# One attention step in each TensorE slot: moving steps, loads and the order of x's chunks

## The chip, the cores and the metric

The kernel runs on one core of one Trainium2 chip. The metric is the device time of one execution in microseconds (us), a median over runs; lower is better.

## What is computed

A landmark attention for 8 batches of 8 heads (576 tokens, 64 wide, 32 landmarks), a feed-forward layer on its output and a second layer with a maximum over three products. q and k are drawn eight times larger than the others.

```python
def _attn_ref(q, k, v):
    q_lm = q.reshape(B, H, m, S // m, D).mean(axis=3)
    k_lm = k.reshape(B, H, m, S // m, D).mean(axis=3)
    A = sm(q, k_lm); Bm = sm(q_lm, k_lm); C = sm(q_lm, k)    # softmax(a b^T / sqrt(D))
    Z = Bm.transpose(0, 1, 3, 2) / (norm1(Bm) * norminf(Bm) + 1e-06)
    for _ in range(6):
        Z = 2 * Z - Z @ Bm @ Z
    return A @ Z @ C @ v

x = attention output as (4608, 512)
h = x @ w_in                                                  # 512 -> 2048
x = where(h > 0, h, exp(min(h, 0)) - 1) @ w_out               # 2048 -> 512
h = maximum(maximum(x @ w1, x @ w2), x @ w3)                  # 512 -> 768
out = h @ w_out2                                              # 768 -> 512
```

(`sm`, `norm1` and `norminf` are shortened here.)

## The kernel before

The first phase does the attention and the first layer, the second phase the layer with the maximum. The first phase is a row of **slots**, 32 to a batch: two halves of 288 tokens, each with 16 values of f, a block of 128 of the 2048 hidden units. Batch b holds slots 32 b to 32 b + 31; below, a slot is named by its place in its batch, 0 to 31. A slot has

- `h_mm` (L667): six matmuls into one of two PSUM buffers `ph`, then on ScalarE a relu and an exp (L671, L672) into `eh`;
- the attention steps that the plan puts into this slot;
- `h_post`: VectorE finishes `eh` (L677), which frees `ph`; ScalarE casts it to the high part of `gt`, GpSimd subtracts for the low part (L103);
- `x_mm` (L698): twelve matmuls for the slot three before, three for each of the four chunks `x0` to `x3` of the output in PSUM. At the end of a half ScalarE copies chunks 0 and 2 and VectorE chunks 1 and 3 to `xo` (L724, L726), and the sync engine (SP) stores them to `xs`.

So the matmul of slot t + 2 waits for `eh` of slot t, and that of x in slot t + 3 for `gt` of slot t.

While batch b - 1 has its 32 slots, the attention of batch b is worked off as small **steps** inside them. `STEP_SLOTS` gives each step its slot, counted from the first slot of batch b - 1 (negative: before it); batch 1 has `SECOND_SLOTS`, `THIRD_SLOTS` overrides four entries of batch 2. The steps are: sums of q and k over landmarks on VectorE (q0, k0, q1, k1; L279), scores c0 and c1, `exp_t` for the two head groups (e0, e1), the product with v (cv0, cv1), the small softmax (b, b2), its norm (nb), `bbt`, six Newton steps n0 to n5, the scores of A (ah0, ah1) with their softmax in three parts (a10 to a31; casts `ah`, subtractions `al`), the small product m, and four W steps (`w_step`, slots in `W_SLOTS`) that make the batch's own first weight `wp`: 16 matmuls, two casts on ScalarE (L639), two subtractions on VectorE (L644).

`exp_t` transposes the exponentials: four chunks of 128 columns by four transposes into one PSUM bank, a copy by ScalarE (L463), then the last chunk of 64 columns into the other bank, and a copy by VectorE (L466). All attention steps share the two banks of the tile `banks`, in turn; every matmul and transpose of a step is issued through a helper, so its line is L235.

In the same slots the second layer's weights are converted. A `Narrowing` loads 1 MB of 64-bit words (L108) into the tile that also holds v, ScalarE widens them (L119, L122), VectorE shifts (L128), GpSimd adds (L131), and SP stores the result (L779). There are two in each of batches 1 to 6.

TensorE and VectorE issue in the order of the program from slot 20 of batch 0 on; ScalarE, GpSimd and SP issue in an order that the scheduler's planner chose when the program was built.

Of the kernel before, what the change touches and what calls it, by code (L numbers as in the profile page):

```python
# [19 lines left out]
def landmark_attention_mlp_maxout_kernel(  # L20
# [24 lines left out]
    CH = -(-S // P)  # L45
# [166 lines left out]
    state = {}  # L212
# [234 lines left out]
    def exp_t(b, g):  # L447
        e = state.pop(("e", b, g))
        if b == 0 and g:
            em = r_s.tile([P, CH - 1, P], F32, tag="gt", name="et", bufs=LAG + 1)  # L450
            el = r_s.tile([P, P], F32, tag="gt", name="et", bufs=LAG + 1)
        else:
            et = att.tile([P, CH, P], F32, tag="et", name="et")
            em, el = et[:, : CH - 1], et[:, CH - 1]
        pt = att_ps(b, "pe")
        for c in range(CH - 1):
            pt.put(
                nc.tensor.transpose,
                pt[:, c * P : (c + 1) * P],
                e[:, c * P : (c + 1) * P],  # L460
                ident,
            )
        nc.scalar.copy(em.rearrange("p c j -> p (c j)"), pt[:])  # L463
        p2 = att_ps(b, "pe")
        p2.put(nc.tensor.transpose, p2[:TAIL, :P], e[:, (CH - 1) * P :], ident)
        nc.vector.tensor_copy(el[:TAIL], p2[:TAIL, :P])  # L466
        state["et", b, g] = [em[:, c] for c in range(CH - 1)] + [el]

    def cv(b, g):
        et, vn, rs = state.pop(("et", b, g)), state["v", b], state["rs", b, g]  # L470
# [213 lines left out]
    def x_mm(b, half, f):  # L684
        gt = gts.pop((b, half, f))

        parts = b == 0
        first = f % (KF // 2) == 0 if parts else f == 0
        last = f % (KF // 2) == KF // 2 - 1 if parts else f == KF - 1
        if b == 0:  # L690
            conv.upto(index["out", f] + 1)
        if first:
            for ec in range(KD):
                xacc[ec] = ps_x.tile([P, 512], F32, tag=f"x{ec}", name=f"x{ec}")
        for ec in range(KD):
# [426 lines left out]
    def att_steps(b):  # L1122

        first = [
            ("q0", lambda: sums(b, 0, "q")),
            ("k0", lambda: sums(b, 0, "k")),
            ("q1", lambda: sums(b, 1, "q")),
            ("k1", lambda: sums(b, 1, "k")),
            ("c0", lambda: score_c(b, 0)),
            ("c1", lambda: score_c(b, 1)),  # L1130
            ("c20", lambda: score_c2(b, 0)),
            ("c21", lambda: score_c2(b, 1)),
            ("e0", lambda: exp_t(b, 0)),
            ("cv0", lambda: cv(b, 0)),
            ("e1", lambda: exp_t(b, 1)),
            ("b", lambda: soft_b(b)),
            ("b2", lambda: soft_b2(b)),
            ("cv1", lambda: cv(b, 1)),
            ("nb", lambda: norm_b(b)),
            ("bbt", lambda: bbt(b)),  # L1140
        ]
        for i in range(6):
            first.append((f"n{i}", lambda i=i: newton(b, i)))
        first += [("ah0", lambda: score_a(b, 0)), ("ah1", lambda: score_a(b, 1)), ("m", lambda: m_step(b))]
        for g in range(2):
            for n, fn in enumerate((soft_a1, soft_a2, soft_a3)):
                first.append((f"a{n + 1}{g}", lambda fn=fn, g=g: fn(b, g)))
        return first


    STEP_SLOTS = dict(
        q0=-10, k0=-9, q1=-8, k1=-6, c0=4, c1=5, b=6, b2=7, c20=8, c21=8, e0=8, nb=9, cv0=10, e1=11,
        ah0=12, cv1=13, bbt=13, ah1=14, n0=15, n1=16, n2=17, n3=18, n4=19, n5=20, m=22,
        a10=15, a11=16, a20=18, a21=19, a30=20, a31=21,
    )
    SECOND_SLOTS = dict(
        q0=3, k0=4, q1=5, k1=6, c0=8, c1=9, c20=11, c21=11, e0=12, b=10, b2=11, cv0=14, e1=15,
        nb=13, ah0=16, cv1=17, bbt=18, ah1=19, n0=20, n1=21, n2=22, n3=23, n4=24, n5=25, m=26,
        a10=20, a11=21, a20=23, a21=24, a30=25, a31=26,
    )  # L1160

    THIRD_SLOTS = dict(q0=-6, k0=-5, q1=-4, k1=-3)
    W_SLOTS = [-7, -5, -2, 1]
    SECOND_W = [-5, -3, -1, 2]

    def load_att(b):
# [71 lines left out]
    for _ in range(NF):  # L1238
# [13 lines left out]
        + [lambda i=i: newton(0, i) for i in range(6)]  # L1252
        + [lambda: m_step(0)],
        "V": [lambda: score_e(0)]
        + [lambda g=g, fn=fn: fn(0, g) for g in range(2) for fn in (score_c2, exp_t)]
        + [lambda g=g: cv(0, g) for g in range(2)],
        "A": [lambda h=h: score_a(0, h) for h in range(2)]
        + [
# [25 lines left out]
    def at(t, fn, *args):  # L1284
        plan[t].append((fn, args))
# [18 lines left out]
    for b in range(1, B):  # L1304
        t0 = (b - 1) * NSL
        if b > 1:
            at(t0 - (12 if b == 2 else 17), load_att, b)
            at(t0, load_v, b)
        for nm, stp in att_steps(b):
            if b > 1:  # L1310
                at(t0 + (THIRD_SLOTS.get(nm) if b == 2 and nm in THIRD_SLOTS else STEP_SLOTS[nm]), stp)
            else:
                at(SECOND_SLOTS[nm], after_post(stp))
        for n in range(NCH):
            at(t0 + NSL + (W_SLOTS if b > 1 else SECOND_W)[n], w_step, b, n)
# [147 lines left out]
```

## Time and profile before

| | us |
|---|---|
| median of 3 runs (1402.71 to 1405.16) | 1402.8 |
| the profiled execution | 1401.64 |
| its span, first to last instruction | 1399.8 |
| batch 0, to its last slot | 167.19 |
| batches 1 to 6 | 97.47, 99.60, 96.68, 96.45, 96.11, 96.30 |
| batch 7 (no attention beside it) | 77.13 |
| second phase | 572.87 |

Busy over the span: TensorE 94%, VectorE 60%, ScalarE 49%, GpSimd 48%. Times in the views count from the span's first instruction. An idle time in brackets is what the engine waited just before the row, and what ended that wait. Batch 3 starts at 364.26, batch 4 at 460.94.

### The profile page before, as it was taken

The numbers are of one execution on the slowest core, as the hardware profiler recorded it, in microseconds if no ns is written. First come the engines' busy times: TensorE is split into PE (matmuls) and PEld (weight loads), VectorE is DVE, ScalarE is ACT, GpSimd is POOL, SyncE is SP. The second block draws the span as 40 slices with busy tenths as digits, with TensorE's granted clock in tenths as the row PEclk, the third lists the DMA queues.
The fourth block names the chain that finished last, engine by engine and source line by source line (L and its number), as shares of the span: only waits on it lengthen the run. The fifth ranks groups of instructions, "written<-read, shape, count | busy, mean of one in ns | idle before, by whom it ended". The sixth has DMA issues, their size and how long they took to land.

```text
span 1399.8 us, 28302 instructions
## 1 busy us (share of the span) xinstructions
PE 1316.2 (94%) x11144; PEld 1233.9 (88%) x11144; DVE 841.9 (60%) x1603; ACT 682.8 (49%) x1555; POOL 677.8 (48%) x671
## 2 busy tenths in 40 slices
PE   4588999998999999999999999899999999999998
PEld 2477889888888888898899999899999999999998
DVE  6885646336346454364453458866777667687673
ACT  4784556555655656555566653322222222245451
POOL 2771424324325334233245457666666666685543
PEclk8698999999999999999999999999999999999999
DMA  9534104222222132041013112221222122249972
GB/s 361 217 108 151 35 19 160 67 72 90 66 99 70 59 130 81 18 161 63 35 63 108 48 63 73 84 97 67 86 109 83 54 110 84 78 151 314 296 246 76
DMA packets 91590, 152.30 MB, mean 109 GB/s; under 512 B 5312, under 2 KB 49472, under 8 KB 91456
## 3 DMA queue, kind: packets, MB, share of 16 engines
q1 hardware_dynamic: 91456, 150.49, 31.3%
q8 instruction: 87, 1.43, 0.4%
q14 instruction: 47, 0.39, 0.1%
HBM read 99.35 MB, written 51.12 MB: 107 GB/s over the span
## 4 chain that ended last, share of the span: by engine, by line
PE 69%; issue 7%; DMA 7%; ACT 6%; POOL 5%; DVE 5%; SPq 0%; POOLq 0%; ACTq 0%; DVEq 0%
PE p L986 24%; PE x L698 22%; PE ph L667 11%; PE p L1095 8%; PE banks L235 5%; DMA words<-in_moe_w_out_dram 3%; DMA words<-in_moe_w_dram 2%; POOL gt L103 1%; ACT words L122 1%; POOL u L854 1%; POOL wf L131 1%; DMA hf<-hs 1%; POOL w L951 1%; ACT eh L671 1%; ACT wf L119 1%
## 5 line engine op out<-in xcount | busy, mean ns | idle before, releaser
L698 PE MATMUL x<-gt,wo 128*128 128x288 f32 x3072 | 469.6, 302 | 11.4 <-DVE xo L726 3.4
L698 PEld LDWEIGHTS x<-gt,wo 128*128 128x128 f32 x3072 | 424.5, 189 | 52.6 <-ACT eh L671 21.8
L986 PE MATMUL p<-xo,w 128*128 128x256 f32 x3402 | 412.3, 284 | 6.9 <-ACT w L949 3.9
L986 PEld LDWEIGHTS p<-xo,w 128*128 128x128 f32 x3402 | 410.2, 191 | 8.9 <-ACT w L949 4.1
L103 POOL TENSOR_TENSOR gt<-eh,gt 128x288 fp32r<-128x288 f32 x243 | 195.9, 811 | 389.5 <-ACT gt L101 363.8
L667 PE MATMUL ph<-ah,wp 128*128 128x288 f32 x1024 | 250.0, 299 | 16.9 <-DVE eh L677 11.0
L667 PEld LDWEIGHTS ph<-ah,wp 128*128 128x128 f32 x1024 | 180.7, 191 | 26.1 <-DVE eh L677 15.7
L854 POOL TENSOR_TENSOR u<-s,v 128x512 f32<-128x512 f32 x99 | 136.2, 1375 | 134.6 <-DVE v L852 134.6
L677 DVE SCALAR_TENSOR_TENSOR eh<-eh,ph 128x288 f32<-128x288 f32 x256 | 113.1, 443 | 133.9 <-ACT eh L672 132.6
L671 ACT ACTIVATE eh<-ph 128x288 f32<-128x288 f32 x256 | 104.3, 409 | 175.9 <-PE ph L667 127.1
L667 PE MATMUL ph<-al,wp 128*128 128x288 f32 x512 | 152.8, 298 | 2.1 <-POOL al L103 2.1
L101 ACT CAST gt<-eh 128x288 fp32r<-128x288 f32 x256 | 109.3, 428 | 75.9 <-DVE eh L677 75.1
L843 ACT COPY s<-p 128x512 f32<-128x512 f32 x99 | 57.9, 585 | 175.2 <-PE p L986 148.5
L1095 PE MATMUL p<-wo,ho 128*128 128x256 f32 x1134 | 138.1, 284 | 4.1 <-ACT ho L1083 3.4
L1095 PEld LDWEIGHTS p<-wo,ho 128*128 128x128 f32 x1134 | 137.3, 192 | 4.8 <-ACT ho L1083 3.8
L672 ACT ACTIVATE eh<-eh 128x288 f32<-128x288 f32 x256 | 113.3, 444 | 5.4
L667 PEld LDWEIGHTS ph<-al,wp 128*128 128x128 f32 x512 | 97.3, 190 | 2.5 <-POOL al L103 2.5
L867 DVE TENSOR_TENSOR t<-p,u 128x512 f32<-128x512 f32 x81 | 55.7, 687 | 65.5 <-POOL u L854 63.2
L644 DVE TENSOR_TENSOR wp<-banks,wp 128x512 fp32r<-128x512 f32 x62 | 39.9, 685 | 76.1 <-ACT wp L639 76.1
L993 DVE TENSOR_TENSOR t<-t 128x1024 f32<-128x1024 f32 x54 | 71.7, 1328 | 9.0 <-POOL t L857 3.9
L1085 DVE TENSOR_TENSOR ho<-hf,ho 128x768 fp32r<-128x768 f32 x54 | 65.9, 1245 | 16.6 <-ACT ho L1083 16.3
L1083 ACT CAST ho<-hf 128x768 fp32r<-128x768 f32 x63 | 51.5, 835 | 42.9 <-PE p L1095 23.4
(167 smaller groups left out, 1421.1 us busy)
## 6 DMA issues: line engine op xcount, KB each, us to landing
hf<-hs SPq DMA_DIRECT2D x63, 384.0 KB, 5.2
hs<-t SPq DMA_DIRECT2D x27, 512.0 KB, 2.6
xs<-xo SPq DMA_DIRECT2D x36, 288.0 KB, 3.2
hs<-s SPq DMA_DIRECT2D x27, 384.0 KB, 2.9
qT<-in_q_dram SPq DMA_DIRECT2D x16, 576.0 KB, 6.1
kT<-in_k_dram SPq DMA_DIRECT2D x16, 576.0 KB, 7.1
words<-in_moe_w_dram SPq DMA_DIRECT2D x9, 1024.0 KB, 6.4
xf<-xs SPq DMA_DIRECT2D x9, 1024.0 KB, 5.0
```

What stands on the lines that cost most here:

```text
L101: nc.scalar.copy(hi, src)
L103: eng.tensor_tensor(out=lo, in0=src, in1=hi.bitcast(F32), op=ALU.subtract)
L235: ins = fn(*args, **kw)
L667: nc.tensor.matmul(ph[:, :HF], a, c, start=(g == 0 and j == 0), stop=(g == 1 and j == 2))
L671: nc.scalar.activation(e, ph[:, :HF], AF.Relu, scale=-1.0)
L672: nc.scalar.activation(e, e, AF.Exp, scale=-1.0)
L677: state["post"] = nc.vector.scalar_tensor_tensor(out=e, in0=e, scalar=1.0, in1=ph[:, :HF], op0=ALU.subtract, op1=ALU.max)
L698: nc.tensor.matmul(xacc[ec][:, :HF], a, gt[:, c], start=(first and j == 0), stop=(last and j == 2),)
L854: nc.gpsimd.tensor_tensor(out=u57, in0=s57, in1=v.unsqueeze(1).to_broadcast([P, 2, 256]), op=ALU.add)
L986: nc.tensor.matmul(dst, l, r, start=(c == 0 and j == 0), stop=(c == 1 and j == 2))
L993: nc.vector.tensor_tensor(out=t, in0=t, in1=cur, op=ALU.max)
L1095: nc.tensor.matmul(dst, l, r, start=(c == 0 and n == 0), stop=(c == NP - 1 and n == 2))
```

## The change

- `exp_t` is cut in two: the last chunk's transpose and its copy become a step of their own, `exp_t2` (t0, t1). In batch 0's own attention, ahead of the slots, the two still follow each other.
- The tables: in batches 2 to 7 no slot holds two steps that issue on TensorE. bbt moves from 13 to 10, cv0 from 10 to 11, e1 to 12, cv1 to 14, the A scores to 16 and 18, the Newton steps to 15, 17 and 19 to 22, m to 24, A's softmax to 19 to 25. The sums of q and k move from 22, 23, 24 and 26 to 24, 25, 26 and 28, the first two W steps from 25 and 27 to 26 and 28. In batch 1 only t0 and t1 are added.
- q and k of batches 3 to 7 are loaded in slot 19 instead of 15. The words are loaded in slots 15 and 23 instead of 13 and 24, and widened four slots later instead of three.
- `x_mm` takes the chunks in the order 0, 2, 1, 3.

```diff
@@ exp_t
+        state["et", b, g] = e, el, [em[:, c] for c in range(CH - 1)] + [el]
         pt = att_ps(b, "pe")
...
         nc.scalar.copy(em.rearrange("p c j -> p (c j)"), pt[:])
+
+    def exp_t2(b, g):
+
+        e, el, state["et", b, g] = state["et", b, g]
         p2 = att_ps(b, "pe")
         p2.put(nc.tensor.transpose, p2[:TAIL, :P], e[:, (CH - 1) * P :], ident)
         nc.vector.tensor_copy(el[:TAIL], p2[:TAIL, :P])
-        state["et", b, g] = [em[:, c] for c in range(CH - 1)] + [el]
@@ x_mm
-        for ec in range(KD):
+
+        for ec in (0, 2, 1, 3):
@@ 
     STEP_SLOTS = dict(
-        q0=-10, k0=-9, q1=-8, k1=-6, c0=4, c1=5, b=6, b2=7, c20=8, c21=8, e0=8, nb=9, cv0=10, e1=11,
-        ah0=12, cv1=13, bbt=13, ah1=14, n0=15, n1=16, n2=17, n3=18, n4=19, n5=20, m=22,
-        a10=15, a11=16, a20=18, a21=19, a30=20, a31=21,
+        q0=-8, k0=-7, q1=-6, k1=-4, c0=4, c1=5, b=6, b2=7, c20=8, c21=8, e0=8, t0=9, nb=9, bbt=10,
+        cv0=11, e1=12, t1=13, cv1=14, n0=15, ah0=16, n1=17, ah1=18, n2=19, n3=20, n4=21, n5=22, m=24,
+        a10=19, a11=20, a20=22, a21=23, a30=24, a31=25,
     )
@@ 
-    W_SLOTS = [-7, -5, -2, 1]
+    W_SLOTS = [-6, -4, -2, 1]
@@ 
-            at(t0 - (12 if b == 2 else 17), load_att, b)
+            at(t0 - (12 if b == 2 else 13), load_att, b)
@@ 
-        t0 = (1 + it // 2) * NSL + (13, 24)[it % 2]
+        t0 = (1 + it // 2) * NSL + (15, 23)[it % 2]
         at(t0, nw.load)
         run = nw.run()
         for n in range(4):
-            at(t0 + 3 + n, next, run, None)
+            at(t0 + 4 + n, next, run, None)
```

**TensorE, slots 8 and 9 of a batch.** `ident,e` are the transposes. First the order before, from the transposes of slot 8 to the next slot's first matmuls:

```order
L235 MATMUL banks<-ident,e 128x128 x4
L235 MATMUL banks<-ident,e 64x128
L698 MATMUL x_2023<-gt,wo 128x288 x3
L698 MATMUL x_2024<-gt,wo 128x288 x3
L698 MATMUL x_2025<-gt,wo 128x288 x3
L698 MATMUL x_2026<-gt,wo 128x288 x3
L667 MATMUL ph<-ah,wp 128x288
```

and TensorE in the same place of the changed kernel, to the lone transpose:

```order
L235 MATMUL banks<-ident,e 128x128 x4
L703 MATMUL x_2023<-gt,wo 128x288 x3
L703 MATMUL x_2025<-gt,wo 128x288 x3
L703 MATMUL x_2024<-gt,wo 128x288 x3
L703 MATMUL x_2026<-gt,wo 128x288 x3
L671 MATMUL ph<-ah,wp 128x288
L671 MATMUL ph<-al,wp 128x288
L671 MATMUL ph<-ah,wp 128x288 x2
L671 MATMUL ph<-al,wp 128x288
L671 MATMUL ph<-ah,wp 128x288
L235 MATMUL banks<-ident,e 64x128
```

The 64-column transpose has moved behind the twelve matmuls of x and the next slot's six.

**ScalarE, around the widening of the second words** (`wf<-words`), from the exp ahead of it. Before, in slot 20, with m's copy (`mt`) and no W step near:

```order
L672 ACTIVATE eh<-eh 128x288
L101 CAST gt<-eh 128x288
L119 ACTIVATE wf_2963<-words_2848 128x512
L122 ACTIVATE words_2848<-words_2848 128x512
L119 ACTIVATE wf_2966<-words_2848 128x512
L122 ACTIVATE words_2848<-words_2848 128x512
L101 CAST ah<-af 128x288 x2
L671 ACTIVATE eh<-ph 128x288
L101 CAST gt<-eh 128x288
L672 ACTIVATE eh<-eh 128x288
L101 CAST ah<-af 128x288 x2
L627 COPY mt<-banks 128x128
```

ScalarE in the changed kernel, in slot 24, to the casts of slot 26's W step (`wp`):

```order
L122 ACTIVATE words_2795<-words_2795 128x512
L101 CAST ah<-af 128x288 x2
L675 ACTIVATE eh<-ph 128x288
L101 CAST gt<-eh 128x288
L676 ACTIVATE eh<-eh 128x288
L101 CAST ah<-af 128x288 x2
L675 ACTIVATE eh<-ph 128x288
L101 CAST gt<-eh 128x288
L676 ACTIVATE eh<-eh 128x288
L643 CAST wp<-banks 128x512 x2
```

The widening now stands two slots ahead of a W step instead of five.

**VectorE, slots 24 to 29**: eh, the sums of q and k (L279), W's subtractions (`wp`), the shift (`wf`). Before:

```order
L279 TENSOR_REDUCE qs<-qT 128x64
L677 SCALAR_TENSOR_TENSOR eh<-eh,ph 128x288
L644 TENSOR_TENSOR wp<-banks,wp 128x512 x2
L677 SCALAR_TENSOR_TENSOR eh<-eh,ph 128x288
L279 TENSOR_REDUCE kT<-kT 128x2x32
L677 SCALAR_TENSOR_TENSOR eh<-eh,ph 128x288
L644 TENSOR_TENSOR wp<-banks,wp 128x512 x2
L677 SCALAR_TENSOR_TENSOR eh<-eh,ph 128x288
L128 TENSOR_SCALAR wf_2963<-wf_2963 128x512
L128 TENSOR_SCALAR wf_2966<-wf_2966 128x512
L677 SCALAR_TENSOR_TENSOR eh<-eh,ph 128x288 x2
```

and VectorE in the changed kernel, from slot 25's eh:

```order
L681 SCALAR_TENSOR_TENSOR eh<-eh,ph 128x288
L648 TENSOR_TENSOR wp<-banks,wp 128x512 x2
L279 TENSOR_REDUCE qs<-qT 128x64
L681 SCALAR_TENSOR_TENSOR eh<-eh,ph 128x288 x2
L648 TENSOR_TENSOR wp<-banks,wp 128x512 x2
L279 TENSOR_REDUCE kT<-kT 128x2x32
L128 TENSOR_SCALAR wf_2945<-wf_2945 128x512
L128 TENSOR_SCALAR wf_2948<-wf_2948 128x512
L681 SCALAR_TENSOR_TENSOR eh<-eh,ph 128x288 x2
```

W's subtractions, a sum and, in slot 28, the shift now stand together ahead of one eh.

## Rows read from the trace of the kernel before

**Rows 1.** Busy by stretch, one batch each (2, 4): stretch, us, engines' busy (instructions), granted clock, DMA

```profile
264.66:364.26 99.60, 93.74 (x828) 84.58 (x827) 47.94 (x119) 55.76 (x139) 34.47 (x42) 1.00 0.24 79
460.94:557.39 96.45, 93.33 (x828) 84.50 (x827) 47.56 (x119) 55.84 (x139) 34.46 (x42) 1.00 0.25 83
```

**Rows 2.** Waits of TensorE, whole span: who waited for whom, total us, times, longest

```profile
PE ph L667 <- DVE eh L677: 11.0, 11, 2.6
PE banks L235 <- ACT et L463: 8.3, 12, 0.9
...
PE x L698 <- DVE xo L726: 3.4, 6, 0.6
```

**Rows 3.** Busy by stretch, slots 8, 9, 10, 13, 15, 19, 22, 27

```profile
483.19:487.02 3.83, 3.15 (x25) 2.92 (x24) 2.58 (x13) 2.11 (x6) 2.20 (x4) 1.00 0.00 0
487.02:489.43 2.41, 2.41 (x20) 2.41 (x19) 1.93 (x8) 0.86 (x2) 0.58 (x1) 1.00 0.00 0
489.43:492.86 3.43, 3.43 (x60) 3.08 (x59) 0.75 (x3) 1.72 (x4) 1.18 (x2) 1.00 0.02 5
499.89:504.22 4.33, 3.92 (x65) 3.50 (x64) 1.48 (x5) 1.11 (x4) 0.80 (x1) 1.00 0.26 61
507.48:510.33 2.85, 2.85 (x24) 2.85 (x23) 0.42 (x1) 2.82 (x8) 0.72 (x1) 1.00 0.77 275
422.66:426.31 3.65, 3.11 (x24) 2.87 (x23) 3.16 (x10) 1.57 (x6) 2.81 (x4) 1.00 0.54 167
431.58:435.51 3.93, 3.12 (x25) 2.55 (x23) 0.51 (x2) 3.93 (x12) 1.84 (x3) 1.00 0.04 13
446.46:450.08 3.62, 3.62 (x36) 2.62 (x35) 0.90 (x3) 2.10 (x5) 1.55 (x2) 1.00 0.02 5
```

**Rows 4.** Timeline of TensorE: start, us, row, [idle before, its end]

```profile
485.26 0.30 PE L235 MATMUL banks<-ident,e 128*64 128x128 f32 x1 [0.68 <-ACT et L463]
...
425.01 1.47 PE L698 MATMUL x<-gt,wo 128*128 128x288 f32 x9 [0.54 <-DVE xo L726]
...
435.51 0.40 PE L667 MATMUL ph<-ah,wp 128*128 128x288 f32 x1 [0.81 <-DVE eh L677]
```

**Rows 5.** Timeline of ScalarE: second words in batches 3 and 2, first words, wp

```profile
430.93 0.69 ACT L119 ACTIVATE wf<-words 128x512 f32<-128x512 f32 x1 [2.36 <-DMA words<-in_moe_w_dram]
...
435.45 0.26 ACT L627 COPY mt<-banks 128x128 f32<-128x128 f32 x1
...
334.28 0.67 ACT L119 ACTIVATE wf<-words 128x512 f32<-128x512 f32 x1 [4.14 <-DMA words<-in_moe_w_dram]
...
506.88 0.68 ACT L119 ACTIVATE wf<-words 128x512 f32<-128x512 f32 x1 [0.72 <-DMA words<-in_moe_w_dram]
...
448.55 1.07 ACT L639 CAST wp<-banks 128x512 fp32r<-128x512 f32 x2
```

**Rows 6.** Timeline of SP's queue: issue of the second and of the first words

```profile
424.42 0.38 SPq L108 DMA_DIRECT2D words<-in_moe_w_dram  x1
...
501.74 0.37 SPq L108 DMA_DIRECT2D words<-in_moe_w_dram  x1
```

**Rows 7.** Timeline of VectorE: eh of slot 16, then slots 18 and 25 to 28

```profile
515.37 0.45 DVE L677 SCALAR_TENSOR_TENSOR eh<-eh,ph 128x288 f32<-128x288 f32 x1
...
420.35 1.15 DVE L128 TENSOR_SCALAR wf<-wf 128x512 uint32<-128x512 uint32 x2
...
445.23 1.34 DVE L279 TENSOR_REDUCE kT<-kT 128x64 f32<-128x1152 f32 x1
...
449.65 1.29 DVE L644 TENSOR_TENSOR wp<-banks,wp 128x512 fp32r<-128x512 f32 x2 [2.72 <-ACT wp L639]
450.86 0.45 DVE L677 SCALAR_TENSOR_TENSOR eh<-eh,ph 128x288 f32<-128x288 f32 x1
451.22 0.76 DVE L128 TENSOR_SCALAR wf<-wf 128x512 uint32<-128x512 uint32 x2
```

**Rows 8.** Timeline of GpSimd, the row beside the shift at 420.35

```profile
420.08 0.81 POOL L103 TENSOR_TENSOR gt<-eh,gt 128x288 fp32r<-128x288 f32 x1 [2.13 <-ACT gt L101]
```

More of the change, by code (lines that the diff above doesn't have):

```diff
@@ L1133, in att_steps @@
             ("e0", lambda: exp_t(b, 0)),
+            ("t0", lambda: exp_t2(b, 0)),
             ("cv0", lambda: cv(b, 0)),
             ("e1", lambda: exp_t(b, 1)),
+            ("t1", lambda: exp_t2(b, 1)),
             ("b", lambda: soft_b(b)),
             ("b2", lambda: soft_b2(b)),
-            ("cv1", lambda: cv(b, 1)),
             ("nb", lambda: norm_b(b)),
             ("bbt", lambda: bbt(b)),
+            ("cv1", lambda: cv(b, 1)),
         ]
@@ L1157, in landmark_attention_mlp_maxout_kernel @@
         q0=3, k0=4, q1=5, k1=6, c0=8, c1=9, c20=11, c21=11, e0=12, b=10, b2=11, cv0=14, e1=15,
-        nb=13, ah0=16, cv1=17, bbt=18, ah1=19, n0=20, n1=21, n2=22, n3=23, n4=24, n5=25, m=26,
+        nb=13, ah0=16, cv1=17, bbt=18, ah1=19, t0=13, t1=16, n0=20, n1=21, n2=22, n3=23, n4=24, n5=25, m=26,
         a10=20, a11=21, a20=23, a21=24, a30=25, a31=26,
@@ L1254, in landmark_attention_mlp_maxout_kernel @@
         "V": [lambda: score_e(0)]
-        + [lambda g=g, fn=fn: fn(0, g) for g in range(2) for fn in (score_c2, exp_t)]
+        + [lambda g=g, fn=fn: fn(0, g) for g in range(2) for fn in (score_c2, lambda b, g: [exp_t(b, g), exp_t2(b, g)])]
         + [lambda g=g: cv(0, g) for g in range(2)],
```

## The prediction

> **What bounds the kernel now.** I read the busy times in stretches first, one stretch for a batch. Batches 1 to 6 take about 96.5 us each, batch 2 99.6, with TensorE busy for some 93.5 of them at a granted clock of 1.00 and every other engine below 60 [rows 1]. So TensorE's own queue sets the time there, and only what makes it wait, or what it must do, counts. Batch 0 (167 us) and the second phase (573 us) are touched only at their edges.
>
> Second, the same view with one slot in each stretch [rows 3]. A slot without an attention step takes 2.41 us (18 matmuls). A step of four 128x128 matmuls makes it 2.85, the product with v 3.43, a W step 3.62. The stretches that don't fit these prices are the slots with two steps (8: 3.83; 13: 4.33), slot 19 (3.65 where a Newton slot is 2.85) and slot 22 (3.93, whose step is again four small matmuls).
>
> Third, what TensorE waited for [rows 2], and the waits in place [rows 4]. The last chunk's transpose stands 0.68 behind ScalarE's copy of the four others, 12 times, 8.3 us in all. In slot 19 the second chunk of x waits 0.54 for VectorE's copy out. At the end of slot 22 the next slot's first matmul waits 0.81 for VectorE's eh, because ScalarE had stood 2.36 us for the second words and made everything behind them late [rows 5].
>
> **What the change takes away**, per batch of 1 to 6 unless said.
>
> Transposes apart: slots 8 and 9 take 3.83 + 2.41 now. Four transposes alone are priced like four Newton matmuls, 2.85. The single one alone lies between a quarter of that step's 0.44 and all of it; I take 0.3, so 2.71, because entering and leaving a step costs too. Saved: 6.24 - 5.56 = 0.68. Slot 11 has the same pair and the same wait (12 waits are two per batch). 2 x 0.67 x 6 = 8.0 us. bbt alone: slot 13 and an empty one take 4.33 + 2.41, cv1 alone and bbt alone 3.43 + 2.85; saved 0.46, six times 2.8. Together **10.8**.
>
> Slot 19's wait: 3.65 - 2.85 = 0.8. In the new table slot 18 has only a score step and VectorE reaches the copies of x right after eh, while fifteen matmuls (15 x 2.41 / 18 = 2.0 us) lie between a chunk's last matmul and its next first. The wait goes even without the new chunk order; the order itself delays both the finish and the next need of each chunk equally, so I price it at nothing in these batches. **4.7**.
>
> Slot 22's wait: 3.93 - 2.85 = 1.08, six times 6.5. Batch 2 takes 99.60 where others take 96.5 [rows 1], since there both words transfers came later (4.14 us of wait instead of 2.36 [rows 5]); q and k now load after the first words have landed and x's store goes out ahead of the second, so I count these 3.1 as gone. **9.6**. Sum of gains: **25.1 us**.
>
> **What it adds.** The same engines now hold other work in other slots, and eh(t) must be done two slots later, when its PSUM buffer is written again.
>
> D, slot 20: VectorE now has a Newton pair, the second softmax pair and the narrowing's shift ahead of eh(20). Before, a Newton and a softmax pair ended 5.04 after their slot's start (515.37 against 510.33 [rows 3, 7]), part of it lateness from the slot ahead. With the shift (1.15) and eh (0.45) that is 6.6 against 2 x 2.85 = 5.7: 0.85 at most, nothing if the lateness is gone. I take 0.45, six times: **2.7**.
>
> F, slot 28: W's subtractions, k1's sum and the second shift now stand ahead of eh(28). The subtractions began 3.19 after a W slot's start and eh stood 1.21 behind them (446.46, 449.65, 450.86); the k sum takes 1.3, the shift 0.76, eh 0.45 [rows 3, 7]. Sum 6.9, against 3.62 + 2.41 = 6.0 until slot 30's first matmul: 0.9. Nothing there is late before, so no slack hides it. If the shift takes its other duration, 1.15, it is 1.3. q and k are summed in batches 1 to 5 only: 5 x 0.9 = **4.5**.
>
> The row of the shift that took 1.15 has a GpSimd subtraction beside it (420.08 [rows 8]); the one of 0.76 has none. The Trainium skill ("SBUF — State Buffer", section "SBUF: two separate sides") says that VectorE and GpSimd share one port pair as an exclusive lock, so that the later one blocks for the whole instruction. By that rule the crowded slot 28, where GpSimd has its own backlog, pays the long shift, F is 1.3 and the sum 2.0 worse. The trace agrees with the direction, not with a full block of 0.81.
>
> E, slot 26: W's subtractions and q1's sum ahead of eh(26). Without lateness that is 3.19 + 1.21 + 1.3 + 0.45 = 6.15 against 6.03: 0.1. But ScalarE widens the second words in slot 24. From the first widening to the end of the second pair of ah casts it took 4.52 (430.93 to 435.45 [rows 5]). ScalarE was free for it 2.26 after its slot's start (430.93 - 2.36 - 426.31), about 2.1 now. If the words are there, it is through 6.6 after slot 24's start; some 1.0 for relu, cast and exp, 1.07 for the wp casts (448.55), 1.21, 1.3 and 0.45 on VectorE make 11.65 against 2.85 + 2.41 + 3.62 + 2.41 = 11.3 until slot 28: 0.35. GpSimd's al subtractions, which hold the eh buffers, add up to 0.4; I take 0.5 plus the wait w for the words. Now w: the words were issued 4.07 after the shift's start (420.35 to 424.42 [rows 6, 7]). The shift starts about 4.8 into slot 20, so the issue is at 8.9 there, slot 24 starts at 11.35, and the transfer takes 5.1 (501.74 to 506.88) to 6.5 (424.42 to 430.93). Landing is 2.6 to 4.0 into slot 24, w is 0.4 to 1.8, and I take the middle, 1.0. E = 1.5, between 0.1 and 2.7; five times 7.5, and 0.2 in batch 6, which has no q1: **7.7**.
>
> The second words again, by a page: the Trainium skill ("DMA: Bandwidth & Descriptors", section "Bandwidth") gives 6.15 us for 1 MB. By that w would be 1.5 and the sum 3 us worse; the rows hold durations on both sides of it.
>
> G, batch 0: there VectorE adds the chunks in the order 0, 1, 2, 3 while TensorE now wants chunk 2 second, a chunk's three matmuls (0.4) earlier: **0.4**, at most twice.
>
> Costed at nothing: cv0, e1, cv1 and the Newton steps a slot later (every step still has its predecessor's result a slot earlier); q and k loaded at slot 19 instead of 15 (the first 0.6 MB is wanted five slots, some 13 us, later, the last nine slots later, and the words' 1 MB takes 6.5 at most); W steps in other slots (same matmuls); the moved stores of x on SP's queue, which nobody waits for until the next half.
>
> **Sum.** 25.1 - 2.7 - 7.7 - 4.5 - 0.4 = 9.8. The profiled execution took 1401.6 and lies 1.2 under the median of 1402.8; 1401.6 - 9.8 + 1.2 = **1393.0 us**.
>
> **Rivals.**
> 1. The words come in time and GpSimd is out of the way: E is 0.1 to 0.35 and the time 1386. For it: with q, k and x's stores elsewhere the words have the queues nearly alone, as in the 5.1 us transfer. Against: the stores of the first narrowing still go just ahead of them. 0.22.
> 2. Slower: the second words land late in every batch as they did in batch 2 (1.8 later than in the others), w is 2.8, E grows by 1.8 six times and the long shift stands in slot 28 (1.75): 1405.6. It decides from w of about 2.6. For it: ScalarE's queue still holds the widening ahead of casts and relus that TensorE needs. Against: that lateness shows in one batch. 0.08.
> 3. The change does not do what it says: the single transpose waits for the copy in its own slot too. 12 x 0.69 come back, 1401.3. Against it: the copy had ended when the transpose started at 485.26 [rows 4], and a lone transpose stands a slot later. 0.04.
> 4. D, E and F all come out at their long ends short of rival 2: 1397 to 1401. 0.16.
>
> **How the numbers follow.** My forecast, 1389 to 1397, has 0.50. With all additions at their low ends it is 1381, with D, E and F long and batch 2's 3.1 still there it is past 1405. The range 1382 to 1401 leaves out rival 2, rival 3's half and the tails, some 0.17. About 0.2% (2.8 us) is what a measurement here can tell: faster than 1400 has 0.86, within 0.2% 0.08 (rival 3 and the worst of 4), slower 0.06.
>
> **What would show it.** Right: no wait of TensorE for L463's copy or for x's copies in slot 19; slots 8, 9 and 10 near 2.85, 2.7 and 2.85; new waits for eh ahead of slots 28 and 30 in batches 1 to 5, none or little in batch 6, a small one ahead of slot 22. Wrong: slots 26 to 30 without any wait (E and F fall, about 1382), a single-transpose slot near 3.4, or a wait of ScalarE for words above 2.5 us.

## The result, and the profile after

The changed kernel takes 1388.3 us (median of 5 runs, 1387.5 to 1391.0), the kernel before in the same runs 1402.7: a ratio of 0.9908, 95% interval 0.9892 to 0.9924. The forecast was 1393.0 us with a range of 1382 to 1401. The profiled execution took 1388.28 us (before 1401.64), its span is 1386.5.

By stretch, in us, batches as in the table of before: batch 0 168.16; batches 1 to 6 96.12, 94.63, 96.65, 94.60, 94.30, 92.21; batch 7 77.15; second phase 572.7. So all of the gain lies in batches 1 to 6, 14.1 us, and 1.0 of it is lost in batch 0. The busy times of batches 4 and 6 (columns as in [rows 1]):

```profile
455.56:550.16 94.60, 92.86 (x828) 84.59 (x827) 47.70 (x119) 55.83 (x140) 34.43 (x41) 1.00 0.25 84
...
644.46:736.67 92.21, 92.21 (x828) 84.39 (x827) 42.96 (x115) 56.24 (x140) 34.52 (x42) 1.00 0.18 63
```

Batch 6, which has no sums of q and k, has no idle time of TensorE left: 92.21 of 92.21. Batch 4 waits 1.74 us in all, where before it waited 3.12 [rows 1]. The same view by slot, of batch 4, answers to [rows 3]: slots 8, 9, 10, 14, 19, 22, 24, 27 and 29.

```profile
477.81:480.66 2.85, 2.85 (x25) 2.85 (x23) 1.66 (x8) 1.69 (x5) 1.26 (x3) 1.00 0.00 0
480.66:483.18 2.52, 2.52 (x21) 2.50 (x20) 1.31 (x8) 1.29 (x3) 1.48 (x2) 1.00 0.00 0
483.18:486.05 2.87, 2.87 (x24) 2.87 (x23) 2.48 (x10) 1.34 (x4) 0.52 (x1) 1.00 0.00 0
494.77:498.20 3.43, 3.43 (x60) 3.08 (x59) 0.64 (x2) 1.72 (x4) 1.18 (x2) 1.00 0.12 19
510.52:513.37 2.85, 2.85 (x24) 2.85 (x23) 1.80 (x5) 1.23 (x4) 0.81 (x1) 1.00 0.94 350
519.08:522.09 3.01, 3.01 (x24) 2.94 (x23) 2.22 (x7) 1.17 (x4) 3.01 (x4) 1.00 0.32 117
524.50:527.46 2.96, 2.96 (x25) 2.62 (x23) 2.89 (x6) 1.76 (x5) 1.08 (x2) 1.00 0.57 219
533.48:537.11 3.63, 2.58 (x20) 2.34 (x18) 2.96 (x5) 1.51 (x5) 0.87 (x2) 1.00 0.00 0
540.83:544.04 3.21, 2.58 (x21) 2.34 (x19) 3.21 (x7) 0.88 (x3) 0.68 (x1) 1.00 0.00 0
```

The slots that lost their second step cost what their step costs, the lone transpose (slot 9) only 0.11 over an empty slot. Slots 19 and 22 have lost their waits but for 0.2 in 22. What is new is at the end: 27 and 29 are empty slots (2.41) that take 3.63 and 3.21, with TensorE busy for 2.58 in both and VectorE for all of slot 29. In batches 1 to 6 slot 27 takes 4.12, 3.85, 4.38, 3.63, 3.45, 2.41, slot 29 3.22, 3.21, 3.13, 3.21, 3.19, 2.41.

The waits of TensorE over the whole span (as [rows 2]) keep one large row of the slots. The rows for ScalarE's copy of the transposes (L463) and for VectorE's copies of x in slot 19 (L726) are gone, and that for eh has grown from 11.0 us to 15.1:

```profile
PE ph L671 <- DVE eh L681: 15.1, 17, 1.8
```

In place, in batch 3, at the end of slots 27 and 29, TensorE's timeline (start, us, row, idle before and what ended it):

```profile
441.07 0.43 PE L671 MATMUL ph<-ah,wp 128*128 128x288 f32 x1 [1.80 <-DVE eh L681]
...
449.44 0.40 PE L671 MATMUL ph<-ah,wp 128*128 128x288 f32 x1 [0.56 <-DVE eh L681]
```

VectorE's timeline there: W's subtractions, q's or k's sum, in slot 28 the shift, and eh last, twice, since it is two behind:

```profile
438.10 1.29 DVE L648 TENSOR_TENSOR wp<-banks,wp 128x512 fp32r<-128x512 f32 x2 [2.66 <-ACT wp L643]
439.31 1.34 DVE L279 TENSOR_REDUCE qs<-qT 128x64 f32<-128x1152 f32 x1
440.57 0.81 DVE L681 SCALAR_TENSOR_TENSOR eh<-eh,ph 128x288 f32<-128x288 f32 x2
...
445.80 1.29 DVE L648 TENSOR_TENSOR wp<-banks,wp 128x512 fp32r<-128x512 f32 x2 [4.43 <-ACT wp L643]
447.01 1.34 DVE L279 TENSOR_REDUCE kT<-kT 128x64 f32<-128x1152 f32 x1
448.27 0.75 DVE L128 TENSOR_SCALAR wf<-wf 128x512 uint32<-128x512 uint32 x2
448.94 0.81 DVE L681 SCALAR_TENSOR_TENSOR eh<-eh,ph 128x288 f32<-128x288 f32 x2
```

What W's subtractions waited for in slot 26 is on ScalarE, whose timeline shows the wait for the second words, smaller than before (2.36, [rows 5]), and a wait for GpSimd:

```profile
430.89 0.67 ACT L119 ACTIVATE wf<-words 128x512 f32<-128x512 f32 x1 [1.20 <-DMA words<-in_moe_w_dram]
...
436.03 0.41 ACT L675 ACTIVATE eh<-ph 128x288 f32<-128x288 f32 x1 [0.49 <-POOL gt L103]
...
437.01 1.06 ACT L643 CAST wp<-banks 128x512 fp32r<-128x512 f32 x2
```

### The profile page after: what moved, and what is told of

Read it like the earlier page. It is cut to its first block, busy times and chain, and to the rows that moved or that the text cites. A ratio compares the mean times of both kernels' runs of the same rounds, so it can differ in the third digit from the quotient of the medians.

```text
span 1386.5 us, 28338 instructions
## 1 busy us (share of the span) xinstructions
PE 1315.8 (95%) x11144; PEld 1235.8 (89%) x11144; DVE 839.5 (61%) x1603; ACT 684.5 (49%) x1555; POOL 678.2 (49%) x671
## 4 chain that ended last, share of the span: by engine, by line
PE 70%; issue 7%; DVE 6%; POOL 6%; DMA 5%; ACT 5%; SPq 0%; POOLq 0%; ACTq 0%; DVEq 0%
PE p L991 24%; PE x L703 21%; PE ph L671 11%; PE p L1100 9%; PE banks L235 5%; DMA words<-in_moe_w_out_dram 2%; DMA words<-in_moe_w_dram 2%; POOL gt L103 1%; POOL u L859 1%; DVE wp L648 1%; ACT words L122 1%; DMA hf<-hs 1%; POOL al L103 1%; ACT wp L643 1%; POOL w L956 1%
## 5 line engine op out<-in xcount | busy, mean ns | idle before, releaser
L671 PE MATMUL ph<-ah,wp 128*128 128x288 f32 x1024 | 252.3, 301 | 20.7 <-DVE eh L681 15.1
L131 POOL TENSOR_TENSOR wf<-wf,words 128x512 uint32<-128x512 uint32 x40 | 54.5, 1377 | 43.0 <-DVE wf L128 41.3
```

What stands on the lines that cost most here:

```text
L671: nc.tensor.matmul(ph[:, :HF], a, c, start=(g == 0 and j == 0), stop=(g == 1 and j == 2))
```

## The experiments

Ten of the eleven kernels are the changed kernel with one edit or a few; e13_before2 is the kernel before with one. Slot lengths and batches are read as above, from one profiled execution each; times are medians, each beside the kernel before in the same runs (1402.8 to 1404.2).

**All five transposes in one slot again** (e1_join).

```diff
-        ... c20=8, c21=8, e0=8, t0=9, nb=9, bbt=10,
-        cv0=11, e1=12, t1=13, cv1=14, ...
+        ... c20=8, c21=8, e0=8, t0=8, nb=9, bbt=10,
+        cv0=11, e1=12, t1=12, cv1=14, ...
```

> The change with the lone transposes put back into the slots of the other four (t0 in 8, t1 in 12); all else as changed. Theory (the transposes' wait was a cost of sharing a slot): slots 8 and 12 go from 2.85 and 2.82 to about 3.8, slots 9 and 13 from 2.52 to 2.41, the wait for L463's copy is back 12 times near 0.68, and the kernel is 12 x 0.87 = 10.4 us slower than the change, about 1399. Rival (the gain came from where the other steps and loads stand): slots 8 and 12 stay under 3.2 and the time within 3 us of the change, 1388 to 1391.

Measured: 1401.9 us, ratio to the kernel before 0.9981 (95% interval 0.9960 to 1.0002): nearly all of the change's gain is lost. Slots 8 and 12 take 3.83 and 3.80, slots 9 and 13 2.41 and 2.38, that is 12.42 where the changed kernel has 2.85 + 2.52 + 2.82 + 2.51 = 10.70: 1.72 a batch, 10.3 us. TensorE's waits have the row of the copy again:

```profile
PE banks L235 <- ACT et L464: 8.1, 12, 0.7
```

The transpose was not what cost; its wait for a copy out of the *other* bank was. The next four kernels that deal with the banks ask why it waits at all.

**The same with the two PSUM banks as two tiles** (e8_join2).

```diff
-    banks = ps_a.tile([P, 2, 512], F32, name="banks")
+    banks = [ps_a.tile([P, 512], F32, tag=f"bk{g}", name="banks") for g in range(2)]
...
-        return Bank(banks[:, turn[0]], turn[0])
+        return Bank(banks[turn[0]], turn[0])
```

> e1_join (all five transposes of a head group in one slot again, slots 8 and 12) with the two PSUM banks as two tiles of one bank each instead of one tile of two. Theory (the lone transpose waits for the copy of the other bank because the two banks are one tile to whatever sets the dependencies, not because they share a slot): no wait of TensorE for L463's copy, slots 8 and 12 at 2.95 to 3.0 instead of 3.83 and 3.80, slots 9 and 13 at 2.41, batch sums as in the changed kernel, 1388 to 1391. Rival (the transpose waits for something that the sharing of the slot brings, such as the port of PSUM or the clock of the copy): slots 8 and 12 stay at 3.8 and the time at 1402.

Measured: 1385.4 us, 0.9881 (0.9855 to 0.9906). The wait is gone although the five transposes share a slot. Slots 8 and 9 of batch 3:

```profile
376.21:379.14 2.93, 2.93 (x25) 2.93 (x24) 1.18 (x7) 1.56 (x4) 2.11 (x3) 1.00 0.02 6
379.14:381.55 2.41, 2.41 (x21) 2.41 (x20) 2.17 (x11) 1.29 (x3) 0.81 (x1) 1.00 0.00 0
```

2.93 + 2.41 is, within 0.03, what the two apart cost (2.85 + 2.52). Batch 0 also became shorter, 162.9 instead of 168.2, which was not expected.

**bbt back beside the second product with v** (e7_bbt).

```diff
-        ... nb=9, bbt=10,
+        ... nb=9, bbt=14,
```

> The changed kernel with bbt back in the slot of the second product with v (slot 14; slot 10 is then empty). Theory of the prediction (two steps in a slot cost what each costs alone plus some 0.46, because the second step's operands and PSUM bank are waited for): slot 10 at 2.41, slot 14 at 4.3, against 2.87 + 3.43 now, +0.4 a batch, six times 2.5 us: 1390.8. Rival (a slot with two steps costs only their matmuls, and the 0.46 read from slot 13 was something else, such as a row of the copy that stood late there): slot 14 at 3.87, sums unchanged, 1388.3.

Measured: 1395.0 us, 0.9942 (0.9923 to 0.9961), 6.6 over the changed kernel where 2.5 were expected. Slot 14 takes 4.47 and slot 10 2.41, against 3.43 + 2.87: 0.58 a batch, 3.5 us. The rest lies in slots 27 and 28, with two falls of the clock against one in the profile of the changed kernel, and in slot 18 of batch 4 (4.04). In slot 14 TensorE's and VectorE's timelines show which wait the 0.5 is:

```profile
402.15 0.61 PE L235 MATMUL banks<-bb,td 128*128 128x128 f32 x4
403.26 0.90 PE L235 MATMUL banks<-v,et 128*32 128x64 f32 x40 [0.50 <-DVE rr L580]
```

```profile
402.79 0.41 DVE L580 SCALAR_TENSOR_TENSOR rr<-banks,rc,eye 128x32 f32<-128x32 f32 x2 [1.47 <-PE banks L235]
```

The product with v takes nothing from L580. It goes into the other bank, and waits until VectorE has read bbt's.

**The same with two tiles** (e12_bbt2: the edits of e7_bbt and e8_join2's of the banks).

> e7_bbt with the two PSUM banks as two tiles. Theory (the second step of a slot waited for VectorE's read of the other bank, 0.50 in e7_bbt's slot 14, because both banks are one tile): no such wait, slot 14 at 3.43 + 2.87 - 2.41 = 3.89 to 3.95 instead of 4.47, slot 10 at 2.41, so the pair of slots costs what the two steps cost apart. With batch 0's gain of 5 us from two tiles 1383 to 1388. Rival (the 0.50 is bbt's own chain of operands): slot 14 stays at 4.4 to 4.5 and the time at 1389 to 1391.

Measured: 1386.1 us, 0.9869 (0.9838 to 0.9899). Slot 14 of batch 3 has no wait left, and 2.41 + 3.90 is, within 0.01, what the two steps cost apart (2.87 + 3.43):

```profile
393.51:397.41 3.90, 3.90 (x64) 3.60 (x63) 1.47 (x5) 1.72 (x4) 1.20 (x2) 1.00 0.15 14
```

**The kernel before with two tiles and nothing else** (e13_before2: the edit of the banks in the old code).

> The kernel before with nothing changed but the two PSUM banks, which are two tiles: all steps in their old slots, two of them in slots 8, 11 and 13. Theory (what the change gained in slots 8 to 14 was the price of a dependency between the two banks, not of two steps in a slot): slots 8 and 11 at 2.94 instead of 3.83 and 3.80, slot 13 at 3.85 to 3.95 instead of 4.33, 0.89 + 0.86 + 0.43 = 2.2 a batch, six times 13 us; batch 0 some 5 less; slots 19 and 22 as before (3.65, 3.9): 1402.8 - 18 = 1385, about the changed kernel's time without any step moved. Rival (the old order has other waits right behind these, VectorE's eh above all, that take over): slots 14 to 18 grow by what 8 to 13 lose and the time is 1395 or above.

Measured: 1388.8 us, 0.9885 (0.9857 to 0.9913): with no step moved, the time of the changed kernel. Slots 8, 11 and 13 of batch 4, which took 3.83, 3.80 and 4.33:

```profile
472.51:475.45 2.94, 2.94 (x25) 2.94 (x24) 1.20 (x7) 1.56 (x4) 2.14 (x3) 1.00 0.00 0
481.28:484.22 2.94, 2.94 (x26) 2.94 (x24) 0.74 (x2) 1.31 (x3) 0.43 (x1) 1.00 0.00 0
487.45:491.31 3.86, 3.86 (x64) 3.51 (x63) 1.48 (x5) 1.10 (x4) 0.81 (x1) 1.00 0.15 38
```

Slots 19 and 22 keep their waits (3.68 and 3.96 in batch 3). Batch 0 came out at 165.9, only 1.3 shorter where 5 were expected; the median lies 3.8 above the expected 1385, the profiled execution (1385.8) does not. Batch 2 lost its late words too, though no load was moved: its second words took 6.45 us from issue to the first widening instead of 8.12, and it takes 94.81 where batches 3 to 5 take 94.42, 94.87 and 94.11. Two steps in a slot are not dear in themselves: the two banks were one tile, and a step that writes one bank was made to wait for the engine that still reads the other.

**The chunks of x in the old order** (e2_order).

```diff
-        for ec in (0, 2, 1, 3):
+        for ec in range(KD):
```

> The change with x's chunks in the order 0, 1, 2, 3 again. Theory (slot 19's wait went because the slots ahead of it hold less for VectorE, not because of the order): in batches 1 to 6 slot 19 stays at 2.83 to 2.85 and nothing else moves; slot 3 of batch 1 falls from 3.67 to about 3.4; time 1388, within 1 us of the change. Rival (the order removed the wait): slot 19 rises by 0.5 to 0.8 in six batches and the time by 3 to 5 us, 1391 to 1393.

Measured: 1392.3 us, 0.9913 (0.9888 to 0.9937), not to be told from the changed kernel. By the time alone that could be the rival's; the slots decide. Slot 19 stays at 2.83 to 2.85 in all batches: its wait left with the plan, not with the order. Slot 3 of batch 1 takes 3.40 instead of 3.67 and batch 0 166.4 instead of 168.2, 2.0 less together in these two profiles; slot 27 was longer (4.24 to 5.00 in batches 1 to 5) and took them back.

**The sums of q1 and k1 away from W's subtractions** (e3_spread).

```diff
-        q0=-8, k0=-7, q1=-6, k1=-4, ...
+        q0=-8, k0=-7, q1=-5, k1=-3, ...
```

> The change with q1's and k1's sums one slot later (27 and 29 instead of 26 and 28), so that neither shares a slot with a W step. Theory (TensorE waits ahead of slots 28 and 30 because W's subtractions, a sum and, in 28, the shift stand together ahead of one eh): slot 27 falls from 3.4 to 4.4 to 2.5 to 2.9 (what the late words leave), slot 29 from 3.2 to 2.4; 4 + 5 to 7 us in batches 1 to 5 and the 1.5 of batch 3's slot 28, so about 1378. Rival (ScalarE's late widening sets it alone): slot 27 stays above 3.2, only slot 29 falls, time about 1384.

Measured: 1378.3 us, 0.9819 (0.9795 to 0.9842). Slots 27 and 29 of batch 3:

```profile
433.27:436.47 3.20, 2.58 (x21) 2.35 (x19) 1.71 (x4) 2.34 (x7) 1.69 (x3) 1.00 0.00 0
440.17:442.58 2.41, 2.41 (x21) 2.41 (x20) 2.41 (x6) 1.22 (x3) 1.01 (x1) 1.00 0.00 0
```

F is gone whole. Slot 27 takes 3.00, 3.25, 3.20, 2.57 and 3.65 in batches 1 to 5, in four of them more than the 2.5 to 2.9 expected. What is left follows the second words: from their issue to the first widening it took 5.91, 6.36, 6.31, 5.65 and 6.74 us, in the same order of size, and slot 27 is 2.91 to 3.11 shorter than that in each. In the changed kernel those are 5.95, 5.75, 6.25, 5.50 and 5.32, and 1.83 to 1.90. So a late transfer comes out one to one in slot 27, and with words equally late the slot is 1.1 to 1.2 shorter, nearly a sum's length (1.34); the slots themselves fell by 0.75 in the mean, since the words came later in this profile.

**The second words widened in slot 29** (e4_widen29, with the sums where the changed kernel has them).

```diff
+    def after_last(run, none):
+        with tc.issue_after(state["exp"].ins):
+            next(run, none)
...
-            at(t0 + 4 + n, next, run, None)
+            at(t0 + (6 if it % 2 else 4) + n, after_last if it % 2 and n == 0 else next, run, None)
```

> The change with the second words widened in slot 29 (held behind that slot's exp) instead of in 24, and the shift in slot 30. Theory: without the widening ScalarE is on time for slot 26's casts, so with q1 still there slot 27 falls to about 2.5, and slot 28 keeps k1 but loses the shift, so slot 29 falls to about 2.5; slot 31 stays near 2.41; time about 1378. Rival (the sums on VectorE alone set slot 27, lateness of ScalarE doesn't matter): slot 27 stays above 3.2 and only slot 29 falls, time about 1384.

Measured: 1387.1 us, 0.9882 (0.9860 to 0.9904), no gain. Slots 27 and 31 of batch 3 (slot 29 took 2.56):

```profile
436.38:439.37 2.99, 2.58 (x21) 2.35 (x19) 2.97 (x5) 0.88 (x3) 0.00 (x0) 1.00 0.00 0
...
449.33:452.75 3.42, 2.57 (x21) 2.34 (x19) 2.38 (x6) 1.89 (x6) 0.68 (x1) 1.00 0.00 0
```

Slot 27 takes 2.98 or 2.99 in each of batches 1 to 5: without the words the stall is the same everywhere, and 0.57 of it remains, W's subtractions and q1's sum. But slot 31 has a new wait of 1.0, since the widening, moved there, now makes slot 30's relu and W's casts late, and the shift stands ahead of eh(30). A load on ScalarE that is moved behind one W step stands before the next. Batches 1 to 6 come out 3.4 shorter all the same; the second phase took 3.9 more in this profile, in code that is not touched, and that I can't explain.

**Sums apart, and the second words widened in slot 25** (e5_widen25: e3_spread and e4_widen29's edit with 2 for 6).

> The spread of the k and q sums as in e3_spread, and the second words are widened one slot later, in slot 25, behind that slot's exp, so that ScalarE no longer stands for them ahead of the casts and exps of slots 24 and 25. Theory (what is left of slot 27's stall in e3_spread, 0.6 to 1.2 us in a batch, follows the words' time from issue to widening): no wait of ScalarE for the second words above 0.3, slot 27 at 2.41 to 2.55 in batches 1 to 5, slot 29 at 2.41; about 0.7 x 5 = 3.5 us less than e3_spread's 1378.3, so 1374 to 1376. Rival (the stall is VectorE's own sum in slot 25 and 26 and GpSimd's subtractions, the words only stand beside it): slot 27 stays at 2.9 to 3.2 and the time at 1378. A second rival: the widening, now nearer to the W step of slot 26, makes its casts late and moves the wait there: slot 27 at 3.2 to 3.6 and 1380 to 1382.

Measured: 1374.3 us, 0.9803 (0.9780 to 0.9826). ScalarE no longer waits for second words in any batch, and slots 27 and 29 of batch 3 have no wait:

```profile
432.14:434.55 2.41, 2.41 (x21) 2.37 (x19) 1.73 (x4) 1.90 (x6) 1.13 (x2) 1.00 0.00 0
438.24:440.65 2.41, 2.41 (x20) 2.41 (x19) 2.41 (x6) 1.24 (x3) 1.03 (x1) 1.00 0.00 0
```

Slot 27 is 2.41 in all six batches. ScalarE's timeline shows the widening with no wait ahead, and W's casts early enough:

```profile
428.14 0.67 ACT L119 ACTIVATE wf<-words 128x512 f32<-128x512 f32 x1
...
431.69 1.09 ACT L643 CAST wp<-banks 128x512 fp32r<-128x512 f32 x2
```

**And with two tiles** (e10_two25: e5_widen25 and the edit of the banks).

> e5_widen25 with the two PSUM banks as two tiles (each step in its own slot, as in the changed kernel). Theory (batch 0, whose steps still crowd one another, gained 5.3 us in e8_join2 because a step there no longer waits for the copy of the other bank; batches 1 to 6 have no such wait left): batch 0 at 163 to 164, batches 1 to 6 as in e5_widen25 (93.5 to 92.2), 1374.3 - 5.2 = 1369. Rival (batch 0's gain in e8_join2 was an order of instructions that happened to come out well there, not the banks): batch 0 at 167 to 168.6 and 1374.

Measured: 1371.8 us, 0.9775 (0.9754 to 0.9797), the shortest time of all. Batch 0 takes 162.4 instead of 168.6, batches 1 to 6 are as in e5_widen25; the second phase, which is not touched, came out 2.8 longer in the profile, so the profiled executions differ by 3.5, and the medians by 2.5, where 5 were expected.

**And the old chunk order, the first shift a slot later** (e11_all).

```diff
-        for ec in (0, 2, 1, 3):
+        for ec in range(KD):
...
-            at(t0 + (2 if it % 2 and n == 0 else 4) + n, ...
+            at(t0 + (2 if it % 2 and n == 0 else 4 if it % 2 or n == 0 else 5) + n, ...
```

> e10_two25 with x's chunks in the order 0, 1, 2, 3 and the first narrowing's shift in slot 21 instead of 20. Theory (D: slot 22's rest of 0.2 is the shift that stands with a Newton pair and a softmax pair ahead of slot 20's eh; G: the new chunk order costs batch 0 and slot 3 of batch 1): slot 22 at 2.85 in batches 1 to 6 with slot 23 still 2.40, slot 3 of batch 1 at 3.40, 6 x 0.2 + 0.3 + up to 1.7 in batch 0, 2 to 3 us less than e10_two25: 1366 to 1367. Rival (the shift only moves its wait a slot on, because slot 21 has a Newton pair too): slot 22 at 2.85 and slot 23 at 2.6, and no more than the chunk order's part is left, 1367 to 1369.

Measured: 1372.8 us, 0.9778 (0.9757 to 0.9799), no gain over e10_two25. Slot 22 did fall to 2.82 with 23 at 2.40, and slot 3 of batch 1 to 3.38, as the theory had it. But batch 0 took 163.8 where e10_two25 took 162.4 and up to 1.7 less was expected, the second phase came out 2.5 longer in the profile, and slot 27 is back at 2.53 to 3.17 in batches 1 to 5: W's first cast comes 5.42 to 6.07 after slot 25's start there, in e10_two25 5.23 to 5.27. Two things stand ahead of it. The first is the words. On SP's queue the stores of the first narrowing stand just ahead of the second words' load. SP's timeline in batch 2, first of e10_two25, whose batch 2 starts at 255.96, then of e11_all, where it starts at 257.21:

```profile
320.05 1.59 SPq L784 DMA_DIRECT2D w2s<-wf  x2
321.69 0.43 SPq L108 DMA_DIRECT2D words<-in_moe_w_dram  x1
```

```profile
323.50 1.60 SPq L784 DMA_DIRECT2D w2s<-wf  x2
325.15 0.43 SPq L108 DMA_DIRECT2D words<-in_moe_w_dram  x1
```

The load is issued 65.7 and 67.9 after the batch's start: the later shift made the stores 2.2 later, and these the load. ScalarE waits for the words 0.14, 0.13 and 0.55 us in batches 1, 3 and 4, and not in 2 and 5, where the widening starts as early as in e10_two25 or earlier (in batch 2 73.7 after the batch's start in both). The second is ScalarE's order: the cast of slot 24's `gt` stands ahead of slot 25's exp in e10_two25 and between the two halves of the widening in e11_all, in batches 1 to 5. ScalarE's timeline in batch 2, first of e10_two25, then of e11_all:

```profile
329.01 0.43 ACT L101 CAST gt<-eh 128x288 fp32r<-128x288 f32 x1
...
329.68 0.67 ACT L119 ACTIVATE wf<-words 128x512 f32<-128x512 f32 x1
```

```profile
330.88 0.67 ACT L119 ACTIVATE wf<-words 128x512 f32<-128x512 f32 x1
...
332.01 0.42 ACT L101 CAST gt<-eh 128x288 fp32r<-128x288 f32 x1
332.33 0.70 ACT L119 ACTIVATE wf<-words 128x512 f32<-128x512 f32 x1
```

In batches 2 and 5 this cast is all that the rows show (slot 27: 2.53 in both); in batch 4, with 0.55 of wait besides, slot 27 is the longest, 3.17. No run separates the two.

## Why the prediction was right, term by term

The time came out 4.7 us below the forecast, in the range and on the side of its gains, but just under the band of 1389 to 1397 that had a chance of 0.50. Three of the prediction's sums are a little off: D is 0.94 at most by its own terms (5.04 + 1.15 + 0.45 against 5.70), not 0.85; without E and F it is 1380.8, not 1382; and with D and E at their low ends and F, which has none, at 4.5, it is 1383, not 1381. The profile of after gives each term its size:

| term | forecast | measured | how |
|---|---|---|---|
| A, transposes and bbt apart | -10.8 | -13.2 | slots 8 to 14, 16, 18: 26.88 against 24.26 + 2 x 2.41, six times |
| B, slot 19 | -4.7 | -5.0 | 3.66 to 2.83, six times |
| C, m's wait and batch 2 | -9.6 | -9.4 | slots 22 and 23 before against slots 24 and 25; batch 2's slots 16, 17 |
| D, slot 22 | +2.7 | +1.3 | 3.05 against 2.83, six times |
| E, slot 27 | +7.7 | +7.4 | 1.71, 1.44, 1.97, 1.22, 1.04, 0 |
| F, slots 28 to 30 | +4.5 | +4.9 | 0.8 in slot 29 and 0.1 each in 28 and 30, five times |
| G, batch 0, slot 3 of batch 1 | +0.4 | +1.3 | 1.0 and 0.3 |
| not priced: Newton slots | | -1.5 | five slots, 14.43 to 14.18 |
| not priced: clock in batch 3 | | +1.5 | slot 28: 5.24 instead of 3.71 |

They add up to -12.7; the profiles differ by 13.4, batches 0 to 7 by 13.1.

**A: the mechanism right, a size off, the reason incomplete.** "I take 0.3" for the lone transpose was the mis-sized term: it cost 0.11 (2.52 over 2.41), a quarter of four, which the prediction had as its lower end. 12 x 0.19 = 2.3 is nearly all that was missing. Why the wait was there at all the prediction took from the row (behind ScalarE's copy) without asking why a write into one bank should wait for a read of the other. e8_join2, e12_bbt2 and e13_before2 answer it: the wait is bound to the tile, not to the slot. Two steps' matmuls in a slot cost, within 0.03, what they cost apart. Rival 3 (the single transpose waits in its new slot too) did not come: no such wait is left.

**B and C: right in size, the causes in part not shown.** The order of x's chunks was costed at nothing in batches 1 to 6, and e2_order shows slot 19 at 2.83 without it; which of the moved steps took its wait away no run separates. Batch 2's late words, counted as gone, are gone: batch 2 takes 94.63 where batches 1 and 4 take 96.12 and 94.60. But the moved loads, which the prediction gave as the reason, need not be it: e13_before2 leaves the loads where they were, and nearly all of the 3.1 us is gone there too. They may have been those of one execution; that this part of the sum came out is then luck.

**D: too large.** The sum had a shift of 1.15 ahead of eh(20); it took 0.75:

```profile
421.05 0.75 DVE L128 TENSOR_SCALAR wf<-wf 128x512 uint32<-128x512 uint32 x2
421.72 0.45 DVE L681 SCALAR_TENSOR_TENSOR eh<-eh,ph 128x288 f32<-128x288 f32 x1
```

eh ended at 422.17, 5.6 after slot 20's start (416.56) instead of 6.6 at worst, and the slot that wants it started at 422.23. So eh(20) cost some 0.1, at slot 22's first matmul; another 0.1 is ahead of the slot's Newton matmuls. The 0.2 together are the shift's: with it a slot later (e11_all) slot 22 takes 2.82 to 2.85.

**E: the sum right, by two errors that cancel.** The wait w for the words was taken as 1.0; ScalarE waited 0.75, 0.70, 1.20, 0.26 and not at all in batches 1 to 5, 0.6 in the mean. The rest was taken as 0.5; the stall less w is 0.96, 0.74, 0.77, 0.96 and 1.04, some 0.9. Without any words it is still 0.57 (e4_widen29). So the crowd of casts and subtractions ahead of eh(26) was under-priced: slot 26's relu waited 0.49 for GpSimd there (436.03, above). Rival 1 (E at 0.1 to 0.35) did not come though its words did in batch 5. The experiments show that the parts do not simply add: the stall, 1.48 in the mean of batches 1 to 5, is 0.72 without q1's sum (e3_spread), 0.57 without the words (e4_widen29) and nothing with the sum and the widening each a slot later (e5_widen25).

**F: right**, with the short shift, 0.75. The condition named for the long one, a subtraction of GpSimd beside it, did not arise in slot 28. e3_spread takes F away by moving k1's sum alone.

**Rival 2** (the second words late in every batch) did not come: the time from issue to widening was 5.3 to 6.25, within the forecast's 5.1 to 6.5.

**G: too small** by 0.9, all of it in batch 0. That the chunk order costs it is not shown: with the old order batch 0 is 1.8 shorter in e2_order, but 1.4 longer in e11_all than in e10_two25.

## What to carry to other kernels

Where an engine waits for the reader of a buffer that it does not write, look whether the two are parts of one tile: two tiles instead of one gave here what moving 22 steps gave (1388.8 and 1388.3 us), and both together, with two sums and a widening one slot later, 1371.8. After steps have been moved apart, read the slots they went to for what now stands together on the next engine: one slot later for two sums on VectorE was worth 10 us. And follow a moved instruction beyond its own slot: a shift one slot later delayed a store and the load behind it by 2.2 us and came with another order of casts on ScalarE, and TensorE paid in a slot six slots on.

## What the runs showed of the hardware

**A wait can be followed by a fall of TensorE's clock, and need not.** In the changed kernel's batch 3 TensorE stood 1.80 us ahead of 441.07 (above). In the slot after that the granted clock is 0.67 in the mean (a stretch at half speed, 1.2 of 2.4 GHz, in it), and a slot of 3.71 takes 5.23:

```profile
441.07:446.30 5.23, 5.23 (x34) 3.29 (x35) 0.80 (x2) 2.70 (x6) 1.56 (x2) 0.67 0.01 3
```

e1_join's batch 1 and e7_bbt's batches 1 and 2 have the same slot at 5.24 and 5.25. In e12_bbt2's batch 3, behind a wait of 2.87, it is 6.38 at a granted clock of 0.53. But in e2_order slot 27 took 4.24 to 5.00, waits as long and longer, and the clock stayed full in batches 1 to 6; in e7_bbt it fell after slots 27 of 4.22 and 4.35 and not after one of 4.83; and in the kernel before a wait of 2.56 in batch 2 left it full. What decides it stays open. Here such a wait had 1.5 us at stake, once 2.7, in some batches, which no sum of durations contains.

**Some of VectorE's work stands behind GpSimd's.** In the prediction I read the shift of 1.15 beside a subtraction as less than a full block. Rows of e11_all, VectorE's and then GpSimd's timeline, show a full one:

```profile
413.37 1.16 DVE L128 TENSOR_SCALAR wf<-wf 128x512 uint32<-128x512 uint32 x2
414.45 0.44 DVE L681 SCALAR_TENSOR_TENSOR eh<-eh,ph 128x288 f32<-128x288 f32 x1
...
415.01 0.74 DVE L423 TENSOR_REDUCE t<-x 128x18 f32<-128x576 f32 x1
415.78 1.22 DVE L424 TENSOR_SCALAR t<-t 128x18 f32<-128x18 f32 x1
```

```profile
413.10 0.81 POOL L103 TENSOR_TENSOR gt<-eh,gt 128x288 fp32r<-128x288 f32 x1 [2.17 <-ACT gt L101]
414.27 2.69 POOL L131 TENSOR_TENSOR wf<-wf,words 128x512 uint32<-128x512 uint32 x2 [0.36 <-DVE wf L128]
```

The small operation at 415.78, which takes 0.18 in the changed kernel's batch 4 (at 521.67), ended at 417.00, when the second of GpSimd's two additions ended (416.96). eh, which has an operand in PSUM, and the reduction at 415.01 ran at their usual 0.44 and 0.74 in the middle of the same addition. The shift had begun 0.27 after the subtraction, with 0.54 of that left, and its first instruction ended 0.28 after the subtraction did; the pair took 0.41 more than the 0.75 it takes alone. Over the whole trace of the changed kernel, each of the 18 instructions of the shift that began while a GpSimd instruction ran ended 0.28 to 0.29 after that one; the 38 others took 0.38 to 0.43. The Trainium skill ("SBUF — State Buffer", section "SBUF: two separate sides") says that of an operation of VectorE in a two-port mode or with two SBUF inputs and one of GpSimd whichever comes first holds the ports for the whole instruction. The trace agrees, if the held forms are of that kind, which no row shows. The price is the rest of the other's instruction, at most the 1.4 us of one addition in these rows.

**Batch 0 was 4 to 6 us shorter with two tiles** in the changed plan (168.2 to 162.9, 168.1 to 163.7, 168.6 to 162.4) and 1.3 in the old one. Where in batch 0 they come from was not followed.
